# Banded attention ahead of two feed-forward blocks: scores on 64 by 64 quarters of the array, row sums by a unit column

## The chip, the cores and the metric

The kernel runs on one core of a Trainium2 chip. The metric is the device time of one execution in microseconds (us). Times are medians over executions; the profile is of one execution.

## The reference

Attention over 2 batches of 8 heads, 768 positions of 64 dimensions. Each query sees the keys less than 16 positions away, and 24 summaries of the whole sequence (the maximum of each block of 32 keys, the mean of each block of 32 values). Two feed-forward blocks follow.

```python
k_sum = k.reshape(B, H, nb, 32, D).max(axis=3)
v_sum = v.reshape(B, H, nb, 32, D).mean(axis=3)
scores_l = where(|i - j| < 16, scale * q @ k.T, -1e9)
scores_s = scale * q @ k_sum.T + log(32)
a = softmax(concatenate([scores_l, scores_s]))      # a / (sum(a) + 1e-9)
x = a @ concatenate([v, v_sum])                     # 1536 rows x 512
x = x / rms(x) * rms_g
x = (silu(x @ w_gate) * (x @ w_val)) @ w_out        # 512 -> 1536 -> 512
x = (s * relu(x @ w_in) ** 2 + b) @ w_out2          # 512 -> 2048 -> 512
```

## The kernel before

**Tiles.** The 1536 rows (2 batches of 768) are 12 tiles of 128 queries, numbered 0 to 11; tiles 0 to 5 are batch 0. A tile has two halves of 64 queries, and each half sees 96 keys of its own window and the 24 summaries: KC = 120 columns of scores for each of 8 heads. The 8 heads are two groups of four, so there are 24 units of work, one for each tile and group.

**Scores (L587).** The two halves of a tile see different keys. On the SBUF partitions the keys of the first half are in rows 0 to 63 and those of the second half in rows 64 to 127. The queries come from DRAM already laid out with zeros (`qz`): for each head a 128 by 128 block, in which one half of the queries has its dimensions in the upper 64 rows and zeros below, the other the reverse. One matrix product of depth 128 for each head then gives 128 queries by 120 scores. Half of `qz` is zeros: 24 loads of 256 KB.

**The rest of a unit.** VectorE adds the mask and takes the row maximum, head by head (`do_top`, L597, tile `P`). ScalarE takes the exponential and with it the row's sum (`do_exp`, L604). TensorE turns the four heads (L615) into a PSUM bank, ScalarE copies that to `PT` (L634), TensorE multiplies with the values (L644). GpSimd makes the reciprocal of the sums (L621, L622, a power of -1), and VectorE multiplies by it (L651) into `xn`. When both units of a tile are there, ScalarE takes the sum of squares (L670), GpSimd its power of -1/2 (L675, L676), VectorE scales the row (L678), TensorE turns it (L686), and ScalarE and VectorE write it as a high and a low part into `x` (L699, L701).

**Summaries.** VectorE reduces the keys (L292), copies halves across (L297), and ScalarE or GpSimd spreads them beside the keys (L303, L305). The means of values are summed on VectorE (L332), turned on TensorE (L345) and copied beside some windows of values (L352, L354); 18 transfers within SBUF (L357) take them to the other windows.

**Feed-forward.** Weights come as pairs of words and are rebuilt on ScalarE, VectorE (L218 to L220) and GpSimd (L235), then split in two parts. A product of one block of weights with 512 rows of `x` is 12 matrix products of 512 columns (`mm12`, L786, L787, L790). The first 6 weights of the first block run in the attention's time, once for each of three blocks of 512 rows (tiles 0 to 3, 4 to 7, 8 to 11): 18 such products. All else follows them, in an order of its own.

**Order of the work.** `plan` lists tasks with an engine, an assumed duration, dependences and a rank, and `give_out` hands them out by a simulated clock: at each moment each free engine takes the lowest rank that is ready. The result is a fixed order on each engine, and on the chip each engine takes its instructions strictly in that order. Where the simulated TensorE would be idle for more than 0.6 us, four transpositions of the identity (L459) are put in its order. PSUM's 8 banks are shared by purpose (`caps`: 3 for scores, `S`).

## Time and profile before

| what | value |
|---|---|
| median of 3 executions | 649.98 us (648.75 to 651.63) |
| the profiled execution, its own time | 650.19 us |
| its span from first to last instruction | 648.4 us |
| TensorE busy | 626.2 us (97%) |
| VectorE, ScalarE, GpSimd busy | 383.0, 269.0, 155.4 us |
| DMA | 59.4 MB, mean 92 GB/s |

The profiled execution took 1.8 us more than its span. A busy time is a share of the whole span, over stages that differ: the attention lies in the first 110 us or so, and TensorE's products of the feed-forward blocks fill the rest.

### The profile page before, as it was taken

What the parts mean: (1) busy time and instruction counts of PE and PEld (TensorE: products, weight loads), DVE (VectorE), ACT (ScalarE), POOL (GpSimd) and SP (SyncE); (2) the same over time, 40 slices, a digit from 0 to 9 for tenths busy, and PEclk for the clock granted to TensorE, in tenths of its full rate; (3) what the DMA queues carried; (4) which work ended last, traced back from release to release, by engine and by line L of the source; (5) the groups of instructions that cost most, each with busy time, mean ns of one, the idle gap of its engine ahead of it and who ended that gap; (6) DMA issues with size and microseconds to landing.
All of it is one profiled execution on the core that took longest, in us unless ns stands there. A gap on an engine that the chain in (4) does not pass through costs nothing.

```text
span 648.4 us, 8708 instructions
## 1 busy us (share of the span) xinstructions
PE 626.2 (97%) x3232; PEld 518.9 (80%) x3232; DVE 383.0 (59%) x754; ACT 269.0 (41%) x615; POOL 155.4 (24%) x187
## 2 busy tenths in 40 slices
PE   4788989999999999999999999999999999999997
PEld 3577877888888888888888888888888888888886
DVE  4589987225861555644556667870388548845532
ACT  3797996233443333211333335542454045404400
POOL 3456884332221111111111111100221022102100
PEclk9999999999999999999999999999999999999999
DMA  9998942003340211111111111121111211110022
GB/s 283 273 300 272 257 152 98 1 0 98 110 139 11 66 65 66 66 65 66 65 66 65 66 66 65 66 91 40 46 53 65 98 64 44 62 59 2 0 98 97
DMA packets 20930, 59.38 MB, mean 92 GB/s; under 512 B 2664, under 2 KB 2920, under 8 KB 20888
## 3 DMA queue, kind: packets, MB, share of 16 engines
q1 hardware_dynamic: 20888, 58.83, 28.0%
q8 instruction: 25, 0.41, 0.3%
q14 instruction: 17, 0.14, 0.1%
HBM read 54.79 MB, written 3.15 MB: 89 GB/s over the span
## 4 chain that ended last, share of the span: by engine, by line
PE 88%; ACT 4%; DVE 3%; DMA 2%; POOL 1%; issue 1%; SPq 0%; DVEq 0%
PE b L786 21%; PE b L790 21%; PE b L787 21%; PE b L910 7%; PE b L912 7%; PE b L909 7%; ACT P L604 2%; PE b L587 2%; DMA qz<-in_q_t_dram 1%; DMA hg<-in_k_t_dram 1%; PE b L644 1%; ACT PT L634 1%; PE b L615 1%; DVE xn L678 0%; PE b L686 0%
## 5 line engine op out<-in xcount | busy, mean ns | idle before, releaser
L235 POOL TENSOR_TENSOR wl<-wa,wh 128x512 fp32r<-128x512 f32 x68 | 89.8, 1327 | 387.0 <-ACT wh L231 313.8
L786 PE MATMUL b<-x,wh 128*128 128x512 f32 x288 | 113.5, 394 | 0.1
L787 PE MATMUL b<-x,wl 128*128 128x512 f32 x288 | 112.3, 390 | 0.0
L231 ACT ACTIVATE wh<-wa 128x512 fp32r<-128x512 f32 x68 | 41.5, 626 | 96.6 <-PE b L912 45.5
L790 PE MATMUL b<-x,wh 128*128 128x512 f32 x288 | 77.7, 392 | 0.0
L910 PE MATMUL b<-wl,hg 128*128 128x512 f32 (+1 forms) x196 | 75.2, 385 | 0.0
L909 PE MATMUL b<-wh,hg 128*128 128x512 f32 (+1 forms) x196 | 75.2, 385 | 0.0
L787 PE MATMUL b<-y,wl 128*128 128x512 f32 x192 | 74.8, 390 | 0.0
L786 PE MATMUL b<-y,wh 128*128 128x512 f32 x192 | 74.8, 390 | 0.0
L891 DVE SCALAR_TENSOR_TENSOR b<-u,sbc 128x512 f32<-128x512 f32 x48 | 50.7, 1056 | 35.6 <-ACT u L890 35.6
L786 PEld LDWEIGHTS b<-x,wh 128*128 128x128 f32 x288 | 54.1, 188 | 11.2 <-ACT x L699 0.2
L787 PEld LDWEIGHTS b<-x,wl 128*128 128x128 f32 x288 | 54.2, 188 | 10.8
L790 PEld LDWEIGHTS b<-x,wh 128*128 128x128 f32 x288 | 53.6, 188 | 10.8
L787 PE MATMUL b<-hg,wl 128*128 128x512 f32 x144 | 56.1, 390 | 0.0
L786 PE MATMUL b<-hg,wh 128*128 128x512 f32 x144 | 56.1, 390 | 0.0
L220 DVE SCALAR_TENSOR_TENSOR wa<-raw,wa 128x512 int32<-128x512 int32 x68 | 52.4, 770 | 2.0
L811 DVE SCALAR_TENSOR_TENSOR hg<-b,bbc,hg 128x512 fp32r<-128x512 f32 x48 | 36.0, 749 | 28.2 <-ACT hg L810 28.2
L912 PE MATMUL b<-wh,hg 128*128 128x512 f32 (+1 forms) x196 | 51.5, 385 | 0.0
L790 PE MATMUL b<-y,wh 128*128 128x512 f32 x192 | 51.3, 390 | 0.0
L810 ACT ACTIVATE hg<-b,bbc 128x512 fp32r<-128x512 f32 x48 | 33.0, 688 | 42.8 <-DVE b L891 42.8
L918 DVE TENSOR_TENSOR part<-b,part 128x512 f32<-128x512 f32 (+1 forms) x37 | 24.4, 673 | 43.4 <-PE b L912 43.4
L219 DVE SCALAR_TENSOR_TENSOR wa<-raw,wa 128x512 int32<-128x512 int32 x68 | 47.4, 697 | 2.0
(94 smaller groups left out, 975.3 us busy)
## 6 DMA issues: line engine op xcount, KB each, us to landing
raw<-in_w_out_dram SPq DMA_DIRECT2D x28, 512.0 KB
raw<-in_w_in_dram SPq DMA_DIRECT2D x16, 512.0 KB
qz<-in_q_t_dram SPq DMA_DIRECT2D x24, 256.0 KB
raw<-in_w_gate_dram SPq DMA_DIRECT2D x12, 512.0 KB
raw<-in_w_val_dram SPq DMA_DIRECT2D x12, 512.0 KB
vt<-in_v_t_dram SPq DMA_DIRECT2D x8, 384.0 KB
hg<-in_k_t_dram SPq DMA_DIRECT2D x5, 576.0 KB
out_dram<-part SPq DMA_DIRECT2D x11, 256.0 KB
```

What stands on the lines that cost most here:

```text
L219: lambda: nc.vector.scalar_tensor_tensor(out=ai, in0=hi, scalar=-0x80000000, in1=ai, op0=ALU.bitwise_and, op1=ALU.bitwise_or),
L220: lambda: nc.vector.scalar_tensor_tensor(out=ai, in0=lo, scalar=29, in1=ai, op0=ALU.logical_shift_right, op1=ALU.bitwise_or),
L231: nc.scalar.activation(out=r(h), in_=a_t[i], func=AF.Copy)
L235: nc.gpsimd.tensor_tensor(out=r(lo), in0=a_t.pop(i), in1=high[i], op=ALU.subtract)
L786: nc.tensor.matmul(ps, r(hi[:, kk * 128:(kk + 1) * 128]), xh, start=kk == 0, stop=False)
L787: nc.tensor.matmul(ps, r(lo[:, kk * 128:(kk + 1) * 128]), xh, start=False, stop=False)
L790: nc.tensor.matmul(ps, r(hi[:, kk * 128:(kk + 1) * 128]), r(act(kk, 1)), start=False, stop=kk == 3)
L811: nc.vector.scalar_tensor_tensor(out=r(dst[1]), in0=ps, scalar=bias, in1=dst[0], op0=ALU.add, op1=ALU.subtract)
L891: after(0, lambda u=u, ps=ps: nc.vector.scalar_tensor_tensor(out=ps, in0=u, scalar=sbc[:, 0:1], in1=u, op0=ALU.mult, op1=ALU.mult))
L909: nc.tensor.matmul(acc, gh, r(ws[e][0][:, cs]), start=e == 0, stop=False)
L910: nc.tensor.matmul(acc, gh, r(ws[e][1][:, cs]), start=False, stop=False)
L912: nc.tensor.matmul(acc, r(ge[e][:, 1]), r(ws[e][0][:, cs]), start=False, stop=e == 3)
```

## The change

- Scores (now L595): the queries come without zeros (`q`, 12 loads of 256 KB, three buffers instead of two). A head's two halves are two products of depth 64, 64 queries by 120 columns each. Even heads go to PSUM partitions 0 to 63 and odd ones to 64 to 127, each half of the tile to a bank of its own, so the four products of a pair of heads lie on the four 64 by 64 quarters of the array. A tile's scores are now one task of 16 products, which needs the keys of all 8 heads, and a unit is now a half of a tile with all 8 heads, no longer a group of heads with both halves. `S` may hold 4 banks, and there are 4 buffers `PT` instead of 2.
- Values have 66 columns for each head, of which two are set to one by GpSimd (`ones_v`): the product with the values (L656) then gives the row's sum in columns 64 and 65. It needs `PT` of both halves. The exponential (L622) no longer sums; ScalarE copies the sums out of PSUM and adds 1e-9 (`do_sum`, L668, 24 of them), and GpSimd takes one power of 8 columns for each tile (L672).
- Loads of values are one contiguous piece each; means are spread by 5 transfers instead of 18; the vectors `rms_g`, `s`, `b` come as one load, already repeated for 128 rows. In `do_top` the masks of the first and the last half differ from the others. In the other lines only numbers moved (L678 is L695, L686 is L703, L701 is L718, L786 is L803, L787 is L804, L790 is L807, L597 is L615, L615 is L633, L634 is L643, L459 is L464).

```diff
+QB = 3
-    RINGS = {"P": 3, "PT": 2, "u": 2, "vs": 1}
+    RINGS = {"P": 3, "PT": 4, "u": 2, "vs": 1}
-    qz = [const.tile([128, 2, GH, 128], F32, name=f"qz{i}") for i in range(2)]
+    qc = [const.tile([128, NH, HQ], F32, name=f"q{i}") for i in range(QB)]
-        nc.sync.dma_start(out=t, in_=v_w[b, :, s0:s0 + n])
+        nc.sync.dma_start(out=t.rearrange("p s h d -> p (s h d)"), in_=v_w[b, s0 // n])
+
+    def ones_v(b, s0, n):
+        rows = KC if s0 < (4 if b == 0 else 2) else KW
+        nc.gpsimd.memset(vst[b][s0 // NTL][0:rows, s0 % NTL:s0 % NTL + n, :, HD:VH], 1.0)
-    caps = {"S": 3, "T": 2, "X": 3, "M": 3}
+    caps = {"S": 4, "T": 2, "X": 3, "M": 3}
-                    VM[b, t, "ok"] = [task("SP", 0.3, lambda s=s: spread_v(b, s), first, 2 * (6 * b + t) - 6) for s in (2 * t, 2 * t + 1)]
+                    if t in (1, 2 if b == 0 else 1, 3):
+                        n = 6 if t == 3 else 2 if b == 0 else 4
+                        spr = task("SP", 0.3 * n, lambda t=t, n=n: spread_v(b, 2 * t, n), [*first, O[b, 0]], 2 * (6 * b + t) - 6)
+                    VM[b, t, "ok"] = [spr]
-        us = [(i, g) for g in range(2) for i in range(2)] + [(i, g) for i in range(2, NT) for g in range(2)]
+        us = [(i, c) for i in range(NT) for c in range(2)]
+            def do_qk(bk):
+                box["S", i, 1] = bank(bk)
+                sm_of[i] = smallp.tile([128, 2, NH], F32, tag="sm", name="sm")
+                for h in range(NH):
+                    j, o = divmod(h, 2)
+                    for c in range(2):
+                        p = slice(64 * c, 64 * c + 64)
+                        nc.tensor.matmul(box["S", i, c][64 * o:64 * o + 64, j * KC:(j + 1) * KC].rearrange("p (r c) -> p r c", c=CH),
+                                         qc[i % QB][p, h], kst[b][h // GH][p, h % GH, :, t], start=True, stop=True)
+            deps = [Q[i], *[o for h in range(NH) for o in KM[b, h]], *([qk[i - 1]] if i else ())]
-                for j in range(GH):
-                    h = GH * g + j
-                    nc.tensor.matmul(ps[:, j * KC:(j + 1) * KC].rearrange("p (r c) -> p r c", c=CH),
-                                     qz[i % 2][:, g, j], kst[b][g][:, j, :, t], start=True, stop=True)
-                                     bias=sm_of[i][:, 0, h:h + 1], accum_out=sm_of[i][:, 1, h:h + 1])
+                                     bias=sm_of[i][:, 0, h:h + 1])
-            ex = [task("ACT", 0.38, lambda j=j, f=do_exp: f(j), [tops[j]], n + 0.5 + j * 0.01) for j in range(GH)]
+            ex = [task("ACT", 0.29, lambda j=j, f=do_exp: f(j), [tops[j]], n + 0.5 + j * 0.01) for j in range(GH)]
+            def do_sum(u, i=i):
+                xv = box["X", i, u][:, 0:GH * VH].rearrange("p (h d) -> p h d", h=GH)
+                nc.scalar.activation(out=sm_of[i][:, 1, GH * u:GH * u + GH].rearrange("p (h o) -> p h o", o=1), in_=xv[:, :, HD:HD + 1],
+                                     func=AF.Identity, bias=tiny[:, 0:1])
+            def do_rc(i=i):
+                nc.gpsimd.tensor_tensor(out=sm_of[i][:, 1], in0=sm_of[i][:, 1], in1=mone, op=ALU.pow)
+            for u in range(2):
+                C.append(task("PE", 0.62, lambda bk, u=u, f=do_pv: f(bk, u), [PTS[i, 0], pt, O[b, t], *VM[b, t, "ok"], *C],
+                              n + 0.2, bank="X", give=(("PT", PTS[i, 0]), ("PT", pt)) if u else ()))
+                U.append(task("ACT", 0.2, lambda u=u, f=do_sum: f(u), [C[u]], n + 0.0))
+            RC = task("POOL", 1.6, do_rc, U, n - 1)
+            for u in range(2):
+                N.append(task("DVE", 0.36, lambda u=u, f=do_norm: f(u), [RC, *N], n + 0.0, free=(C[u],), take=() if u else ("xn",)))
```

Three places show how the order of work moves. The first is the start of TensorE's order, before: `hg` and `kx` are buffers of keys (heads 0 to 3 and 4 to 7 of batch 0), `qz_103` and `qz_104` the queries of tiles 0 and 1, `vt` sums of values, `b` a PSUM bank.

```order
L587 MATMUL b_198<-hg,qz_103 128x120 x4
L587 MATMUL b_204<-hg,qz_104 128x120 x4
L459 MATMUL b_219<-ident 128x128 x4
L345 MATMUL b_228<-ident,vt 128x128 x2
L459 MATMUL b_236<-ident 128x128 x4
L615 MATMUL b_248<-ident,P 120x128 x4
L459 MATMUL b_263<-ident 128x128 x4
```

And in the changed kernel, from the last of 7 groups of identity transpositions on, through the scores of tile 0 (8 products on `hg`, 8 on `kx`, `q_102` being the queries of tile 0):

```order
L464 MATMUL b_246<-ident 128x128 x4
L464 MATMUL b_253<-ident 128x128 x4
L464 MATMUL b_263<-ident 128x128 x4
L348 MATMUL b_271<-ident,vt 128x128 x2
L595 MATMUL b_277<-hg,q_102 64x120
L595 MATMUL b_278<-hg,q_102 64x120
...
L595 MATMUL b_277<-kx,q_102 64x120
L595 MATMUL b_278<-kx,q_102 64x120
...
L595 MATMUL b_300<-hg,q_103 64x120
L595 MATMUL b_303<-hg,q_103 64x120
```

The first scores stood first in the order; now they stand behind the turn of the second pair of sums of values (L348), and tile 0 has all 8 heads there at once, where heads 4 to 7 came behind ten other entries.

The second place is VectorE's order ahead of the first scaling of a row (L678, L695: tile 0), before (`b_373` to `b_441` are products with the values of tiles 0 and 1, `b_427` is a bank of scores of tile 2, ISA rows of `sm` alone read out an accumulator):

```order
L651 TENSOR_TENSOR xn<-b_373,sm 128x256
L651 TENSOR_TENSOR xn<-b_388,sm 128x256
L651 TENSOR_TENSOR xn<-b_412,sm 128x256
L597 ISA P,sm<-b_427,mask_97 128x120
L597 ISA sm 128x1
...
L651 TENSOR_TENSOR xn<-b_441,sm 128x256
...
L678 SCALAR_TENSOR_TENSOR xn<-xn,ss,gbc 128x512
```

And in the changed kernel (`b_351` holds scores of tile 2, `b_403` and `b_423` tile 0's products with the values, `b_478` and `b_494` scores of tile 3):

```order
L615 ISA P,sm<-b_351,mask_98 128x120
L615 ISA sm 128x1
L664 TENSOR_TENSOR xn<-b_403,sm 128x256
L664 TENSOR_TENSOR xn<-b_423,sm 128x256
L615 ISA P,sm<-b_478,mask_98 128x120
...
L615 ISA P,sm<-b_494,mask_98 128x120
...
L695 SCALAR_TENSOR_TENSOR xn<-xn,ss,vec 128x512
```

Both multiplications by the reciprocal (L664) now stand together, behind 24 maxima (tiles 0 to 2), and four maxima of tile 3 stand between them and the scaling.

The third place is TensorE's order where the second block of 512 rows begins its products (before: L786 on `b_1370`; `qz_104` is here tile 11's queries):

```order
L587 MATMUL b_1316<-hg,qz_104 128x120 x4
L686 MATMUL b_1328<-ident,xn 128x128 x4
L644 MATMUL b_1336<-part,PT 64x64 x8
L615 MATMUL b_1353<-ident,P 120x128 x4
L587 MATMUL b_1361<-hg,qz_104 128x120 x4
L786 MATMUL b_1370<-x,wh 128x512
L787 MATMUL b_1370<-x,wl 128x512
...
L644 MATMUL b_1385<-part,PT 64x64 x8
```

And in the changed kernel (`b_1541` is the same product, `b_1519` and `b_1595` turn the rows of tiles 8 and 9, `b_1578` turns the first half of tile 11):

```order
L595 MATMUL b_1494<-hg,q_104 64x120
L703 MATMUL b_1519<-ident,xn 128x128 x4
L656 MATMUL b_1527<-part,PT 64x66 x8
L803 MATMUL b_1541<-x,wh 128x512
L804 MATMUL b_1541<-x,wl 128x512
...
L656 MATMUL b_1552<-part,PT 64x66 x8
...
L633 MATMUL b_1578<-ident,P 120x128 x4
L807 MATMUL b_1541<-x,wh 128x512 x4
L703 MATMUL b_1595<-ident,xn 128x128 x4
```

The scores of tile 11 stand just ahead in both. Before, three units were still to be turned and four still to be multiplied with the values from the first L786 of this product on; now two and three.

## Rows read from the trace of the kernel before

**Rows 1.** Busy time by stretch of the span: stretch and length, then each engine's busy us
```profile
0.00:20.50 20.50, 10.48 (x50) 7.57 (x50) 10.88 (x41) 8.97 (x31) 7.98 (x34) 1.00 0.94 296
20.50:34.00 13.50, 10.44 (x114) 8.94 (x115) 7.43 (x41) 9.19 (x40) 4.53 (x8) 0.89 1.00 237
34.00:52.70 18.70, 16.26 (x194) 14.03 (x192) 16.60 (x55) 15.98 (x54) 12.63 (x19) 0.99 0.93 323
52.70:94.60 41.90, 38.55 (x377) 32.65 (x377) 37.81 (x146) 37.50 (x138) 32.74 (x46) 1.00 0.80 229
94.60:648.40 553.80, 550.48 (x2503) 455.66 (x2501) 310.30 (x475) 197.35 (x355) 97.53 (x82) 1.00 0.18 62
```

**Rows 2.** TensorE in order of time: four marks (start us, us, what, idle before)
```profile
20.54 2.05 PE L587 MATMUL b<-kx,qz 128*128 128x120 f32 x16
...
30.55 1.60 PE L587 MATMUL b<-kx,qz 128*128 128x120 f32 x8 [2.52 <-DMA qz<-in_q_t_dram]
...
52.75 0.50 PE L786 MATMUL b<-x,wh 128*128 128x512 f32 x1
...
94.60 0.48 PE L786 MATMUL b<-x,wh 128*128 128x512 f32 x1
```

**Rows 3.** The same view: scores, a transposition and a value product, each with what follows
```profile
34.03 2.18 PE L587 MATMUL b<-hg,qz 128*128 128x120 f32 x16
36.05 1.06 PE L587 MATMUL b<-kx,qz 128*128 128x120 f32 x8
...
37.38 0.60 PE L615 MATMUL b<-ident,P 128*120 128x128 f32 x4
37.81 0.60 PE L686 MATMUL b<-ident,xn 128*128 128x128 f32 x4
...
45.24 0.69 PE L644 MATMUL b<-hg,PT 120*64 120x64 f32 x16
45.86 0.77 PE L615 MATMUL b<-ident,P 128*120 128x128 f32 x4
```

**Rows 4.** Waits between 52.7 and 94.6 us: TensorE's longest (total, times, longest us)
```profile
PE b L686 <- DVE xn L678: 1.8, 2, 1.5
```

**Rows 5.** VectorE in order of time, 0 to 110 us
```profile
33.89 0.75 DVE L678 SCALAR_TENSOR_TENSOR xn<-xn,ss,gbc 128x512 f32<-128x512 f32 x1
...
57.04 0.74 DVE L678 SCALAR_TENSOR_TENSOR xn<-xn,ss,gbc 128x512 f32<-128x512 f32 x1
57.70 0.94 DVE L292 TENSOR_REDUCE ks<-hg 128x24 f32<-128x768 f32 x1
...
61.28 0.95 DVE L332 TENSOR_REDUCE vs<-vt 128x24 f32<-128x768 f32 x1
62.14 0.42 DVE L651 TENSOR_TENSOR xn<-b,sm 128x256 f32<-128x256 f32 x1
62.47 0.68 DVE L219 SCALAR_TENSOR_TENSOR wa<-raw,wa 128x512 int32<-128x512 int32 x1
63.07 0.28 DVE L597 CUSTOM_DVE_ANT_0 P<-b,mask 128x120 f32<-128x120 f32 x1
63.27 0.69 DVE L220 SCALAR_TENSOR_TENSOR wa<-raw,wa 128x512 int32<-128x512 int32 x1
...
66.90 1.58 DVE L220 SCALAR_TENSOR_TENSOR wa<-raw,wa 128x512 int32<-128x512 int32 x1
```

**Rows 6.** VectorE in order of time, 74 to 115 us: tile 8's scaling
```profile
91.23 0.75 DVE L678 SCALAR_TENSOR_TENSOR xn<-xn,ss,gbc 128x512 f32<-128x512 f32 x1 [0.72 <-POOL ss L676]
```

**Rows 7.** ScalarE in order of time: one exponential, its sum, the next
```profile
70.28 0.39 ACT L604 ACTIVATE P<-P,sm 128x120 f32<-128x120 f32 x1
70.57 0.19 ACT L604 ACTIVATION_READ_ACCUMULATOR P<-P,sm 128x1 f32 x1
70.66 0.39 ACT L604 ACTIVATE P<-P,sm 128x120 f32<-128x120 f32 x1
```

**Rows 8.** GpSimd in order of time: powers of 4 and of 1 columns, a subtraction
```profile
16.27 1.07 POOL L622 TENSOR_TENSOR sm<-sm,mone 128x4 f32<-128x4 f32 x1
...
31.07 0.56 POOL L676 TENSOR_TENSOR ss<-ss,mhalf 128x1 f32<-128x1 f32 x1
...
66.19 1.74 POOL L770 TENSOR_TENSOR hg<-u,hg 128x512 fp32r<-128x512 f32 x1
```

**Rows 9.** SyncE's queue in order of time: spreading the means (issues)
```profile
27.68 6.21 SPq L357 DMA_DIRECT2D hg<-hg  x6
...
75.50 9.72 SPq L357 DMA_DIRECT2D part<-part  x10
```

More of the change, by code (lines that the diff above doesn't have):

```diff
@@ L57, with kernel @@
 @with_exitstack
-def kernel(ctx: ExitStack, tc: tile.TileContext, q_t, k_t, v_w, v_t, w_gate, w_val, w_out, w_in2, w_out2, rms_g, s2, b2, out):
+def kernel(ctx: ExitStack, tc: tile.TileContext, q_t, k_t, v_w, v_t, w_gate, w_val, w_out, w_in2, w_out2, vecs, out):
     nc = tc.nc
@@ L546, in means @@
                 pairs = slice(2 * g, 2 * g + 2)
-                sums = [task("DVE", dve(768), lambda pr=pr: sum_vt(b, pr), [VT[b, pr], z], rank + 1.5 * g,
-                             give=(("raw", VT[b, pr]),) if b else ()) for pr in (2 * g, 2 * g + 1)]
+                sums = [task("DVE", dve(768), lambda pr=pr: sum_vt(b, pr), [VL[b, pr], z], rank + 1.5 * g,
+                             give=(("raw", VL[b, pr]),) if b else ()) for pr in (2 * g, 2 * g + 1)]
                 tv = task("ACT", 0.54, lambda pairs=pairs: turn_vs(b, pairs), sums, rank + 1.5 * g)
@@ L576, in plan @@
+        PTS = {}
         for n, (i, g) in enumerate(us):
             b, t = divmod(i, NTL)
-            if g == 0 and i >= 2:
-                lq(i, (n - 5, n - 4.9), [qk[i - 2, 0], qk[i - 2, 1]])
-            def do_qk(bk, i=i, g=g, b=b, t=t):
-                ps = box["S", i, g] = bank(bk)
-                if i not in sm_of:
-                    sm_of[i] = smallp.tile([128, 2, NH], F32, tag="sm", name="sm")
-                for j in range(GH):
-                    h = GH * g + j
-                    nc.tensor.matmul(ps[:, j * KC:(j + 1) * KC].rearrange("p (r c) -> p r c", c=CH),
-                                     qz[i % 2][:, g, j], kst[b][g][:, j, :, t], start=True, stop=True)
@@ L589, in plan @@
-            deps = [Q[i, g], *[o for j in range(GH) for o in KM[b, GH * g + j]]]
-            A = qk[i, g] = task("PE", 0.82, do_qk, deps, n + 1.2, bank="S", take=("sm",) if g == 0 else ())
+            if g == 0:
+                holds = tile_of(n, i)
+            A, A1 = holds[g], holds[1]
             def do_top(j, i=i, g=g, t=t):
@@ L690, in plan @@
             if i == 2 * TPS:
-                deps += [qk[j, 1] for j in range(NTL)]
+                deps += [qk[j] for j in range(NTL)]
             ET = task("PE", 0.44, do_e, deps, n - 1, bank="M", give=(("xn", box["N0", i]),))
@@ L943, in _layout @@
     c = np.ascontiguousarray
-    qt = np.zeros((NB, NTL, 2, HD, NH, 2, HQ), np.float32)
-    for h in range(2):
-        qt[:, :, h, :, :, h] = q.reshape(NB, NH, NTL, 2, HQ, HD)[:, :, :, h].transpose(0, 2, 4, 1, 3)
-    qt = qt.reshape(NT, 128, 2, GH * 128)
+    qt = q.reshape(NB, NH, NTL, 2, HQ, HD).transpose(0, 2, 3, 5, 1, 4).reshape(NT, 128, NH * HQ)
     own = np.arange(HQ) + WIN
```

146 lines of the change are left out of this document (68 added, 78 removed).

## The prediction

> **What bounds the kernel now.** I first cut the span where TensorE's work changes its kind [rows 1, 2]. At 20.54 us the scores of heads 4 to 7 begin, at 52.75 the first product of the feed-forward block, at 94.60 the second block of 512 rows. From there to the end TensorE is busy 550.48 of 553.8 us: nothing in that stretch can be shortened by attention, so the change can only move the moment at which TensorE reaches that point, and the little attention that is still left behind it. Everything is decided in the first 94.6 us.
>
> There no single engine is the bound. From 52.7 to 94.6 TensorE is busy 38.55 of 41.9 us, VectorE 37.81, ScalarE 37.50, GpSimd 32.74 [rows 1]. TensorE waits for little, and most of it for VectorE's scaling of a row (1.8 us in two waits [rows 4]). From 34 to 52.7 VectorE is busy 16.60 of 18.7. Before 34 everything waits for keys and queries: DMA's share is 0.94 and 1.00, VectorE is busy about half, and TensorE stood 2.52 us for queries at 30.55 [rows 1, 2]. So I read this as three engines, each near nine tenths, in strict orders; what counts is the work that stands ahead of TensorE's second block on each of them.
>
> **The change, part by part.**
>
> *Scores on TensorE.* Sixteen passes of the old scores take 36.05 - 34.03 = 2.02 us, 0.126 us each; a product is two passes, so 96 products cost 192 x 0.126 = 24.2 us [rows 3]. Now there are 192 products, 384 passes. The trace has no pass on a quarter. The nearest row is the value product, whose two halves already lie on two column halves of the array: 16 passes of 64 columns in 45.86 - 45.24 = 0.62 us, 0.039 us each [rows 3]. Lower bound: a quarter's pass costs that too, 384 x 0.039 = 15.0 us, 9 less. Upper bound: four quarters run in turn and each pass costs the old 0.126: 48.4 us, 24 more. A middle one scales the value pass by its columns, 120/64 x 0.039 = 0.073: 28 us, 4 more. I take 0.05 (19 us, 5 less), nearer to the value row, because that row shows that parts of the array overlap, and here four products lie on four parts and two banks.
> The Trainium skill (TensorEngine Tiling, Key Properties) says that tiles execute in parallel, which agrees with the value row; by it alone scores would come to about half of before. The same section says that a change of tiling mode drains the engine; that speaks against the change, which enters and leaves the mode once for each of 12 tiles, and no row here gives its price; what it may cost stands with the rivals.
>
> *Exponentials.* One takes 70.66 - 70.28 = 0.38 us with its sum, of which the read of the sum is the last 0.09 (it starts at 70.57) [rows 7]. Without the sum I take 0.29: 96 x 0.09 = 8.6 us less. Added are 24 copies of sums out of PSUM, which I price between the 0.09 of such a read and the 0.29 of an exponential, at 0.2: 4.8 us. ScalarE gains 4 us of the 72 that it is busy ahead of 94.6 [rows 1], no more.
> The Trainium skill (ScalarE: Activation LUTs, What ACT_TABLE_LOAD costs) lets a bias read per partition, which both the exponential and the new copy have, add about 93 ns to an instruction; by that the 0.29 stays, as I took it, and with a cheaper exponential it would be a larger gain.
>
> *GpSimd.* A power of 4 columns took 1.07 us, of one column 0.56 [rows 8]: 0.17 a column, so 8 columns cost about 1.75. 24 powers of 1.07 become 12 of 1.75, 25.7 us become 21; the 24 additions ahead of them go, and 12 small settings of ones come. But the reciprocal now starts only when both halves have been multiplied with the values and their sums copied; before it ran beside the turning and the copy. One tile's way from maxima to scaling grows by the sum copies and the power, 2 us, and in the order of GpSimd the power of the next tile stands behind the scaling's power of this one.
>
> *DMA.* 24 loads of 256 KB become 12: 3.1 MB, at the 237 to 323 GB/s of the early stretches [rows 1] 10 us of DMA. VectorE, TensorE and ScalarE hide nearly all of it after 34 us; ahead of that it takes away the 2.52 us wait [rows 2] and about 0.9 us (one 256 KB load) ahead of the keys of heads 4 to 7. The 18 spreads, 6 of which held SyncE's queue for 6.21 us and 10 for 9.72 [rows 9], become 5; TensorE's waits name none of them, so I price this at nothing; if a spread came late, tile 1's or tile 7's value products would stand behind it. The contiguous values and the single load of vectors I price at nothing for the same reason: the loads of values were not waited for.
>
> *The order.* The first scores stand behind the second pair of sums of values and need all keys. So the 4 heads of tiles 0 and 1 that were done by 20.54 come later: TensorE and ScalarE lose that start, VectorE 8 maxima (8 x 0.20 = 1.6 us).
>
> **The sum.** It goes by VectorE, the busiest of the waiting engines in both stretches from 34 to 94.6. Its instructions start after one another, in a row without gaps, by: maximum 0.20, multiplication (L651) 0.33, scaling 0.66, reduction of 768 0.86, one step of weights (L219, L220) 0.60 [rows 5]; the short step L218 I take at 0.34, `x` and the gate's steps at 0.60, small copies at 0.18 and copies of means at 0.42.
> 1. Tile 0's scaling starts at 33.89 before [rows 5]. Now: keys complete at about 19.7 (20.54 less 0.9), scores of a tile 1 us, first maximum at 21. Then 8 maxima 1.6, last exponential 0.4, two turns 0.9 (37.81 - 37.38 = 0.43 each [rows 3]), two copies and the exponentials of tile 1 between them 2.5, value products 1.2, sums 0.4, power 1.75, two multiplications 0.7, squares and their power 1.6: 11. It starts at about 32.5, between 30.5 and 34.5, and ends 0.7 later.
> 2. From there to the last maximum of tile 11's first half, VectorE now has, counted in its order: 65 maxima (13.0), 18 multiplications (5.9), 9 short and 16 long steps of weights (12.7), 9 writes of `x` and 6 gate steps (9.0), 8 reductions (6.9), 8 scalings (5.3), 6 copies (1.5): 54.3 us. Before, from the end of tile 0's scaling to the end of tile 8's (34.6 to 92.0 [rows 5, 6]), it had 46.0 us by the same prices (59, 14, 6 and 12, 7 and 4, 8, 8, 6) in 57.4: 11.4 us went into gaps and into instructions that GpSimd stretched (1.58 us for a step of 0.60 while a subtraction of 1.74 ran [rows 5, 8]). GpSimd has about as many of these subtractions ahead as before, some 8, so 6 us of it stay; the gaps, 5, shrink as TensorE and ScalarE have less to do. I take 9 in all: 63.3 us, and 33.2 + 63.3 = 96.5. The exponential and its wait add 0.8: TensorE turns tile 11's first half at 97.3.
> 3. Behind that: the 553.8 us of before, less one turn (0.43) and one value group (0.62) that are now done earlier, less what stands between the second block's first product and this turn: 8 products at 0.22 (550.48 us over 2503 [rows 1]) and a value group, 2.4. That leaves 550.3.
> Span: 97.3 + 550.3 = 647.6, against 648.4: 0.8 us less. The profiled execution took 650.19 around its span, 0.2 above the median 649.98, so the forecast is a median of 649.2, which I call no change. A half per cent, 3.25 us, is about what a measurement of this kernel tells from no change.
>
> **The rivals.**
> *A larger gain.* The gaps of VectorE nearly vanish, since TensorE (5 us less of scores in the stretch at the lower bound), ScalarE and the queues all give way. With 5 us in place of 9, and tile 0's scaling at 31.5: 5 us earlier, a span of 642.6, median 644.2. For it: VectorE's busy share can be full where its order is filled, and rows 4 show that TensorE waits for it. Against: ScalarE keeps 95% of its work. Chance 0.32.
> *VectorE gets no faster.* The same share of gaps as before, 46.0 in 57.4, makes 67.8 out of 54.3: 101.8 with step 1 and the 0.8, span 652.1, median 653.7. The mechanism is the longer way through GpSimd to the scaling: if each of 8 tiles waits 0.5 us more, it is reached. Chance 0.13.
> *Quarters in turn: slower.* From 52.7 on 6 tiles of scores stand ahead of the second block, 192 passes. TensorE has 3.35 us free in that stretch [rows 1], gives up 96 old passes (12.1) and takes on two turns and three value groups more (2.7). So 192 p - 12.1 + 2.7 > 3.35 from p = 0.066 us on: from there TensorE is the bound. At 0.126 that is 11.4 us over, of which the later end that I forecast hides 2.7: some 8 or 9 more, median 658. A price on each change between the whole array and quarters would act in the same place: at 0.05 a pass the three terms come to 0.2, so 3.15 us stay for 12 changes in this stretch, and from 0.26 us each on TensorE is the bound. Chance of both 0.11. (The drain of the Trainium skill, cited above, is that mechanism.)
> *The change does nothing where it counts:* the scores' gain falls wholly into waits. That is the forecast's own neighbourhood and is in its chance.
>
> **Chances and range.** The forecast, with gaps and stretching between 6.5 and 12, runs from 646.7 to 652.2 by median, which is also its own range, and has 0.44, all of it within the half per cent. The larger gain makes faster 0.32, the two slow rivals slower 0.24. To leave out no more than 2 in 10 it must take in most of the larger gain and of the rival without faster VectorE, and of the quarters in turn only the near end: 643 to 655.
>
> **What the changed profile would show.** Scores: 32 passes of a tile in 1.2 to 1.9 us; over 2.3 and the rival of the turns holds. The first L595 near 20, the first L695 near 32.5, the turn of tile 11's first half (L633, the last but one) near 97. Exponentials 0.29 apart. VectorE over 92% busy from 52 to 95. TensorE idle 8 us more than before ahead of that turn, nearly all of it ahead of 21 us and in waits for L615, L622 or L695; none named after the spreads. The prediction is wrong if TensorE's waits in that stretch name the sums or the power (L668, L672), or if the products of the second block have gaps.

## The result, and the profile after

The changed kernel takes 658.59 us (median of 4 executions, 658.19 to 659.63) against 650.2 us for the kernel before (4 executions): a ratio of 1.0146 (95% interval 1.0124 to 1.0167; the plain quotient of the two medians is 1.0129). It is slower by 8.4 us, on the other side of the forecast and outside its range. The profiled execution took 658.19 us, with a span of 656.4 us; that of before had 648.4.

The stretches of [rows 1], with the last one up to the new end (columns as there):

```profile
0.00:20.50 20.50, 7.36 (x27) 4.96 (x28) 10.98 (x26) 4.80 (x15) 5.50 (x32) 1.00 0.92 288
20.50:34.00 13.50, 12.64 (x190) 9.97 (x191) 6.25 (x51) 10.09 (x33) 2.25 (x6) 1.00 1.05 220
34.00:52.70 18.70, 14.43 (x228) 11.02 (x222) 15.88 (x52) 14.22 (x40) 9.92 (x16) 1.00 1.05 314
52.70:94.60 41.90, 37.77 (x420) 29.59 (x421) 37.40 (x130) 33.21 (x94) 22.22 (x30) 0.92 0.61 172
94.60:656.40 561.80, 558.71 (x2600) 457.87 (x2600) 314.28 (x498) 201.90 (x366) 100.90 (x81) 1.00 0.19 61
```

Over the first four stretches together no engine is busier than before (TensorE is in the second, ScalarE in the second too). The loss shows when the same point of the work is looked for in both: the 300th matrix product of the feed-forward blocks starts at 157.70 us before and at 160.55 after, and from there to the end it takes 490.7 and 495.85 us. So 2.85 of the 8.0 us of span are lost in the attention and 5.15 behind it, in a stretch that the forecast held to be unchanged.

TensorE in order of time, answering to [rows 2, 3]:

```profile
13.27 8.10 PE L464 MATMUL b<-ident 128*128 128x128 f32 x28
...
22.06 1.08 PE L595 MATMUL b<-hg,q 64*64 64x120 f32 x16
...
54.63 0.63 PE L703 MATMUL b<-ident,xn 128*128 128x128 f32 x4 [2.09 <-DVE xn L695]
...
57.14 0.80 PE L803 MATMUL b<-x,wh 128*128 128x512 f32 x1 [0.63 <-ACT x L716]
...
65.30 0.65 PE L633 MATMUL b<-ident,P 128*120 128x128 f32 x4
65.88 1.05 PE L595 MATMUL b<-hg,q 64*64 64x120 f32 x32
66.86 0.69 PE L656 MATMUL b<-hg,PT 120*64 120x66 f32 x16
...
72.24 0.65 PE L633 MATMUL b<-ident,P 128*120 128x128 f32 x4
72.65 0.48 PE L803 MATMUL b<-x,wh 128*128 128x512 f32 x1
...
106.94 0.60 PE L633 MATMUL b<-ident,P 128*120 128x128 f32 x4
```

The scores themselves did what was wanted: 32 passes take 66.86 - 65.88 = 0.98 us, 0.031 each, against 0.126 before. The first product of the blocks starts at 57.14 instead of 52.75. VectorE's first maximum and first scaling, answering to [rows 5]:

```profile
24.02 0.28 DVE L615 CUSTOM_DVE_ANT_0 P<-b,mask 128x120 f32<-128x120 f32 x1 [1.02 <-PE b L595]
...
37.55 0.75 DVE L695 SCALAR_TENSOR_TENSOR xn<-xn,ss,vec 128x512 f32<-128x512 f32 x1
```

Up to that 300th product TensorE's time can be balanced. The view by stretch (columns as in [rows 1]), of before and then of after: all work, then the instructions of two source lines alone, identity transpositions and scores (of those the first two columns, TensorE and its weight loads, are to be read):

```profile
0.00:157.70 157.70, 138.79 (x1071) 114.64 (x1072) 103.92 (x342) 96.88 (x319) 77.88 (x128) 0.99 0.58 175
0.00:157.70 157.70, 7.17 (x44) 5.46 (x44) 0.99 0.58 175
0.00:157.70 157.70, 28.38 (x192) 25.52 (x192) 0.99 0.58 175
```
```profile
0.00:160.55 160.55, 138.14 (x1295) 109.09 (x1296) 105.54 (x342) 92.18 (x247) 63.22 (x105) 0.98 0.54 154
0.00:160.55 160.55, 15.33 (x76) 10.53 (x76) 0.98 0.54 154
0.00:160.55 160.55, 13.99 (x384) 11.36 (x384) 0.98 0.54 154
```

Scores gave back 28.38 - 13.99 = 14.4 us. Transpositions of the identity, put in where the plan left TensorE idle, took 8.2 of it, and TensorE stands idle 22.4 us instead of 18.9. In the same view the products with the values take 17.72 us instead of 16.03, and the three lines of the blocks' 300 products together 2.8 more, since part of them ran at half clock (last section). So most of what scores gave up went into filling and waiting, and some into slower work.

### The profile page after: what moved, and what is told of

It reads as the page before. It is cut to its first block, busy times and chain, and to the rows that moved or that the text cites. A ratio compares the mean times of both kernels' runs of the same rounds, so it can differ in the third digit from the quotient of the medians.

```text
span 656.4 us, 8987 instructions
## 1 busy us (share of the span) xinstructions
PE 630.9 (96%) x3456; PEld 513.4 (78%) x3456; DVE 384.8 (59%) x754; ACT 264.2 (40%) x543; POOL 140.8 (21%) x164
## 4 chain that ended last, share of the span: by engine, by line
PE 90%; DMA 4%; DVE 2%; ACT 1%; issue 1%; SPq 0%; POOL 0%; ACTq 0%
PE b L803 22%; PE b L807 21%; PE b L804 21%; PE b L929 7%; PE b L926 7%; PE b L927 7%; DMA raw<-in_w_val_dram 2%; DMA part<-in_v_w_dram 2%; DMA vt<-in_v_t_dram 1%; PE b L464 1%; PE b L656 1%; PE b L595 1%; PE b L633 1%; DVE P L615 1%; ACT P L622 0%
## 5 line engine op out<-in xcount | busy, mean ns | idle before, releaser
L803 PE MATMUL b<-x,wh 128*128 128x512 f32 x288 | 114.6, 398 | 0.6 <-ACT x L716 0.6
L804 PE MATMUL b<-x,wl 128*128 128x512 f32 x288 | 113.2, 393 | 0.0
L807 PE MATMUL b<-x,wh 128*128 128x512 f32 x288 | 78.3, 394 | 0.0
L926 PE MATMUL b<-wh,hg 128*128 128x512 f32 (+1 forms) x196 | 76.2, 390 | 0.0
L804 PE MATMUL b<-y,wl 128*128 128x512 f32 x192 | 74.7, 389 | 0.0
L803 PE MATMUL b<-y,wh 128*128 128x512 f32 x192 | 74.7, 389 | 0.0
L908 DVE SCALAR_TENSOR_TENSOR b<-u,vec 128x512 f32<-128x512 f32 x48 | 50.7, 1057 | 36.6 <-ACT u L907 36.6
L803 PEld LDWEIGHTS b<-x,wh 128*128 128x128 f32 x288 | 54.6, 190 | 12.1 <-ACT x L716 1.0
L804 PEld LDWEIGHTS b<-x,wl 128*128 128x128 f32 x288 | 54.7, 190 | 10.9
L807 PEld LDWEIGHTS b<-x,wh 128*128 128x128 f32 x288 | 54.0, 190 | 11.1
L803 PE MATMUL b<-hg,wh 128*128 128x512 f32 x144 | 56.7, 394 | 0.0
L804 PE MATMUL b<-hg,wl 128*128 128x512 f32 x144 | 56.5, 392 | 0.0
L929 PE MATMUL b<-wh,hg 128*128 128x512 f32 (+1 forms) x196 | 52.9, 392 | 0.0
L828 DVE SCALAR_TENSOR_TENSOR hg<-b,vec,hg 128x512 fp32r<-128x512 f32 x48 | 36.0, 749 | 28.2 <-ACT hg L827 28.2
L807 PE MATMUL b<-y,wh 128*128 128x512 f32 x192 | 51.3, 389 | 0.0
L827 ACT ACTIVATE hg<-b,vec 128x512 fp32r<-128x512 f32 x48 | 33.0, 687 | 42.8 <-DVE b L908 42.8
```

The costliest lines, as they stand in the source:

```text
L803: nc.tensor.matmul(ps, r(hi[:, kk * 128:(kk + 1) * 128]), xh, start=kk == 0, stop=False)
L804: nc.tensor.matmul(ps, r(lo[:, kk * 128:(kk + 1) * 128]), xh, start=False, stop=False)
L807: nc.tensor.matmul(ps, r(hi[:, kk * 128:(kk + 1) * 128]), r(act(kk, 1)), start=False, stop=kk == 3)
L828: nc.vector.scalar_tensor_tensor(out=r(dst[1]), in0=ps, scalar=bias, in1=dst[0], op0=ALU.add, op1=ALU.subtract)
L908: after(0, lambda u=u, ps=ps: nc.vector.scalar_tensor_tensor(out=ps, in0=u, scalar=sbc[:, 0:1], in1=u, op0=ALU.mult, op1=ALU.mult))
L926: nc.tensor.matmul(acc, gh, r(ws[e][0][:, cs]), start=e == 0, stop=False)
```

## The experiments

**The stretch behind the attention.** Theory: a line of the change that the forecast did not price. Windows of values with 66 columns need 3168 columns in a buffer, and the five buffers `hg` later hold the hidden layers of the blocks:

```diff
-        return hgp.tile([128, NSUB * 2 * SUB], F32, tag="hg", name="hg")
+        return hgp.tile([128, VT], F32, tag="hg", name="hg")
```

That is 3072 columns before and 3168 now. A group of 12 products that read `hg`, from its first product to the next group's (before, then after):

```profile
291.21 0.39 PE L786 MATMUL b<-hg,wh 128*128 128x512 f32 x1
...
293.93 0.39 PE L786 MATMUL b<-hg,wh 128*128 128x512 f32 x1
```
```profile
292.39 0.40 PE L803 MATMUL b<-hg,wh 128*128 128x512 f32 x1
...
295.17 0.40 PE L803 MATMUL b<-hg,wh 128*128 128x512 f32 x1
```

2.72 against 2.78 us. From 140 us on the mean distance of starts of all such products is 226.7 ns before and 232.0 after; products that read `x` or `y` stand 226.7 apart in both. The trace has 996 on `hg`: 996 x 5.3 ns = 5.3 us, which is the 5.15 found above. The rival is that the products are slower for the order or for TensorE's clock. Two runs, one from each side:

```diff
 # pad_hg, the changed kernel:
-        return hgp.tile([128, VT], F32, tag="hg", name="hg")
+        return hgp.tile([128, 3584], F32, tag="hg", name="hg")[:, 0:VT]
 # before_wide_hg, the kernel before (a scratch buffer is made smaller for room, as in the changed kernel):
+        return hgp.tile([128, 3168], F32, tag="hg", name="hg")[:, 0:NSUB * 2 * SUB]
```

> The changed kernel with one edit: each tile hg is allocated with 3584 columns and only its first 3168 are used. No instruction moves. Layout theory: the feed-forward products that read hg on either side (996 of them, 432 of the first block's output and 564 of the second's) stand 232.0 ns apart in the changed kernel and 226.7 ns in the kernel before, where the tile had 3072 columns; products that read x or y stand 226.7 ns apart in both. If the place of the tiles in a partition does that, 3584 columns (a multiple of 512, as 3072 is) give 226.7 ns back, 996 x 5.3 ns = 5.3 us: 653.3 us. Rival, all of the loss lies in the attention (late first scores and GpSimd's waits): 658.6 us, and the spacing stays at 232. A second rival, the spacing comes from the memory that the change moved elsewhere (weights and x also lie at other places): the spacing stays too.

> The kernel before with one edit, the converse: tiles hg of 3168 columns instead of 3072, of which 3072 are used (and, to make room, the same small DMA scratch that the changed kernel has). Layout theory: products that read hg go from 226.7 to about 232 ns apart, 5.3 us more, 655.5 us, with the attention as it was. Rival, the loss lies in the attention alone: 650.2 us.

Beside the kernel before at 649.03, pad_hg took 653.28 (1.007, 1.0048 to 1.0093) and before_wide_hg 654.26 (1.0085, 1.0051 to 1.012). A stretch in which TensorE is busy throughout, in the order before, after, pad_hg, before_wide_hg:

```profile
140.00:620.00 480.00, 480.00 (x2119) 397.76 (x2118) 281.15 (x416) 177.04 (x305) 78.83 (x60) 1.00 0.18 63
```
```profile
140.00:620.00 480.00, 480.00 (x2099) 394.08 (x2098) 279.21 (x413) 176.11 (x304) 78.99 (x61) 1.00 0.19 62
```
```profile
140.00:620.00 480.00, 480.00 (x2119) 397.50 (x2118) 282.05 (x418) 177.17 (x305) 78.86 (x60) 1.00 0.18 62
```
```profile
140.00:620.00 480.00, 480.00 (x2099) 394.26 (x2098) 279.25 (x413) 176.73 (x305) 78.84 (x60) 1.00 0.18 62
```

In equal time and at a granted clock of 1.00, the two kernels with 3168 columns do 2099 products and the two others 2119. In the profiled executions of all twenty kernels of this case the stretch from the 300th product of the blocks to the end takes 490.5 to 490.7 us, except for the four with 3168 columns (the changed kernel, before_wide_hg and the next two, ones_loaded and no_early_fill), where it takes 495.8 to 496.0. The size of the buffer alone, without a change of order, gives and takes the 5.3 us: this is shown. (Beside its own kernel before, the changed kernel's excess falls only from 8.4 to 4.2 us, because that kernel took 649.03 beside pad_hg and 650.2 beside the changed kernel.) By which property of an address it acts is open; 3072 and 3584 columns are multiples of 512, 3168 is not, and `x` and `y` lie elsewhere too, without effect.

**GpSimd's ones and the early transpositions.** Padded, the kernel is still 4.2 us over. In the changed kernel's list of waits between 20 and 106 us (total, times, longest us) the first and the third are GpSimd's settings of ones behind loads of values:

```profile
POOL hg L285 <- DMA hg<-in_v_w_dram: 18.3, 5, 7.5
...
POOL part L285 <- DMA part<-in_v_w_dram: 8.9, 5, 3.4
```

Theory: powers that stand behind them come late. In ones_loaded the ones come with the values, and GpSimd sets only the rows of the means, early. A second theory is that the 28 transpositions at 13.27 us keep scores from starting; in no_early_fill none is put in before the first scores.

```diff
 # ones_loaded
-        rows = KC if s0 < (4 if b == 0 else 2) else KW
-        nc.gpsimd.memset(vst[b][s0 // NTL][0:rows, s0 % NTL:s0 % NTL + n, :, HD:VH], 1.0)
+        nc.gpsimd.memset(vst[b][s0 // NTL][KW:KC, s0 % NTL:s0 % NTL + n, :, HD:VH], 1.0)
+    vw[..., HD:VH] = 1.0
```

> The changed kernel with the ones coming in with the loaded values; GpSimd sets only those of the summary rows, early and without a wait for a load. Theory of GpSimd's waits: in the changed kernel GpSimd stands 33.6 us in 11 waits for value loads, with powers queued behind them. For tile 0 the last such wait ends at 32.05, only 0.4 us after tile 0's sums are there; for tile 3 it holds the row's power from 51.7 to 52.9. So tile 0's scaling comes 0.4 us earlier, tile 3's 1 to 1.5, and the first feed-forward product at about 55.6 instead of 57.14: 1 to 2.5 us less, 656 to 657.6 us. What I held right after the result, that these waits are nearly the whole loss, would give 651 to 652. Rival, the start and the longer way through the sums set all: under 0.5 us, 658.1 to 658.6 us.

> The changed kernel without transpositions of the identity ahead of the first scores (28 of them, 8.10 us, end at 21.4, while the last spread of keys ends at 20.66). Theory of the late start: first scores at 20.7 to 21.0 instead of 22.06, first maximum 1 to 1.3 us earlier, tile 0's scaling too: 0.8 to 1.5 us less, 657.1 to 657.8 us. Rival, those transpositions were what brought TensorE's clock up, and without them scores and turns run longer at the lower level: no gain or up to 1.5 us more, 658.6 to 660 us.

ones_loaded took 659.76 (1.0163): no gain, the theory fell. VectorE, GpSimd and TensorE there, at the scaling of tile 3:

```profile
52.54 0.95 DVE L294 TENSOR_REDUCE ks<-hg 128x24 f32<-128x768 f32 x1
53.41 1.29 DVE L694 SCALAR_TENSOR_TENSOR xn<-xn,ss,vec 128x512 f32<-128x512 f32 x1
```
```profile
52.16 0.54 POOL L692 TENSOR_TENSOR ss<-ss,mhalf 128x1 f32<-128x1 f32 x1
52.88 1.26 POOL L234 TENSOR_TENSOR wl<-wa,wh 128x512 fp32r<-128x512 f32 x1 [0.18 <-DMA q<-in_q_t_dram]
```
```profile
54.84 0.63 PE L702 MATMUL b<-ident,xn 128*128 128x128 f32 x4 [2.17 <-DVE xn L694]
```

GpSimd's power is done at 52.70, yet the scaling that TensorE waits for starts at 53.41: here it stands behind a reduction in VectorE's own order. It then takes 1.29 us instead of the usual 0.75, while GpSimd, freed from its wait, runs a subtraction. In the changed kernel this scaling waited 0.36 us for the power, started at 53.73 and took 0.75: it ended at 54.48, here at 54.70. no_early_fill took 656.81 (1.0124); its first scores start at 20.88 instead of 22.06. How large its gain is stays unclear: 1.8 us by the medians, but only 0.6 if each is taken against the executions of the kernel before that stood beside it (7.8 us over 649.03 against 8.4 over 650.2), where 0.8 to 1.5 was expected.

**The rest, from the changed kernel's side.** All these have the padded `hg`. Two further edits are combined with no_early_fill's: `recip` replaces the GpSimd power by VectorE's reciprocal, which shortens the way from sums to scaling, and `halves` gives the scores of tiles 0 and 1 in two tasks, heads 0 to 3 as soon as their keys are there.

```diff
-                nc.gpsimd.tensor_tensor(out=sm_of[i][:, 1], in0=sm_of[i][:, 1], in1=mone, op=ALU.pow)
+                nc.vector.reciprocal(sm_of[i][:, 1], sm_of[i][:, 1])
...
+            A1 = task("PE", 0.5, do_qk, [*deps, A0], rk, bank="S", take=("sm",))
+            A2 = qk[i] = task("PE", 0.5, lambda: do_qk(None, range(NH // 2, NH)),
```

> Both edits that gave time back, together: tiles hg of 3584 columns and no transpositions of the identity ahead of the first scores. They act in different stretches, so they should add: 653.3 less 1.8 = 651.5 us (650.7 to 652.3). Rival, the earlier start was worth something only by chance of where TensorE's clock fell (it stood at 0.50 from 57 to 63 us in the changed kernel, not in the one with padded tiles): 653 us.

> As the run above it, and the reciprocal of the 8 sums by VectorE in place of GpSimd's power. Theory of the longer way through GpSimd: from tile 1 on the power of a tile (1.65 us) starts only when the row's power of the tile ahead is done, that one waits for the squares, these for the multiplication, and this for the power: a ring of about 4 to 6 us a tile, and the rows of tiles 0 to 3 are turned at 39.3, 43.4, 48.5, 54.6 in the changed kernel (36.9, 37.8, 44.0, 51.4 before). Without the power in it tile 0 is 1.5 us earlier and each further one up to 1: the first product 2 to 4 us earlier, 648 to 650 us in all. Rival, VectorE's and ScalarE's orders and the loads set the pace and the ring only fills gaps: under 0.7 us, 650.8 to 651.5 us.

> As the first of these, and the scores of tiles 0 and 1 in two tasks each, heads 0 to 3 as soon as their keys are there (about 5 to 13 us, as before), heads 4 to 7 when theirs are; the maxima of the first two pairs of heads follow the first task. Theory that the late first scores (which now need the keys of all heads) cost: VectorE has 8 of its first 16 maxima, 1.6 us, behind it and ScalarE 8 exponentials, 2.3 us, when the keys of heads 4 to 7 come, so tile 0's scaling comes 1.5 to 2.5 us earlier, 649 to 650.5 us. Rival, TensorE's later start at the low clock or the order behind eats it: 651 to 651.5 us.

> All of the edits above together. If the late start and the way through GpSimd are both causes, it is 646 to 648.5 us, faster than the changed kernel by 10 to 12 and than the kernel before by 1 to 3. If only one is, 648 to 650. If neither, 651.

Beside 648.62 they took 653.08 (1.0055), 652.32 (1.0046), 652.77 (1.0055) and 652.36 (1.0058); every interval excludes 1.002 and none reaches the expected gain. pad_nofill did not add up, and 653.08 is where its rival (653) put it, whose mechanism, the clock, this run does not show. In its profiled execution, at 656.80 the slowest of ten, tile 3's queries came late, a wait that the changed kernel has at 1.34 us; that explains this execution, not the median:

```profile
40.00 1.08 PE L595 MATMUL b<-hg,q 64*64 64x120 f32 x16 [3.81 <-DMA q<-in_q_t_dram]
```

Four more: pad_all has all of these, a fourth buffer of queries and later loads of batch 1's values; pad_all_warm is that with the threshold for identity transpositions at 0.3 us instead of 0.6; pad_old_loads takes back the loads and spreads of before; pad_three_undone is padded, with halves, recip and the old loads.

```diff
-QB = 3
+QB = 4
-            lv(1, t, 9 + t)
+            lv(1, t, 12.5 + 1.5 * t)
-IDLE = 0.6
+IDLE = 0.3
```

> The changed kernel with tiles hg of 3584 columns, no early transpositions of the identity, scores of tiles 0 and 1 in two tasks, VectorE's reciprocal, and two edits to the order of loads: a fourth buffer for queries, so that tile 3's load no longer waits for tile 0's scores (it was waited for 1.3 to 3.8 us), and batch 1's values later in the queue, so that the weights of the first products come ahead of them (a weight was waited for 3.2 us in the last of the runs with halves and reciprocal). If loads are what ate the gains of the other edits, 646 to 649 us; if not, 651 to 653 as those runs.

> The run with all edits (pad_all, 653.05 us; 649.35 in the execution whose granted clock was 1.00, up to 657.94 in those at 0.99), with transpositions of the identity put in where the planner sees 0.3 us of idle time instead of 0.6. If the clock at the first feed-forward products is what spoils it, fewer executions fall below 0.995 and the median comes to 649 to 651; if these transpositions do not hold the clock, or delay work, 653 or more.

> The changed kernel with tiles hg of 3584 columns and the transfers as before: values in pieces of two slots out of a longer row, 18 spreads of means, three loads of the vectors. If the transfers cost as much here as they did on the kernel before (3.0 us), 650 to 651 us; if something else covers them, as with the edits that gave single causes back, 652.5 to 653.5.

> As the run above it, and the scores of tiles 0 and 1 in two tasks (first heads early) and the reciprocal on VectorE: all three parts that cost time on the kernel before undone, with the quarters, the unit column and the cheaper exponentials kept. If these three are the rest of the loss, 646 to 649 us, at the kernel before or ahead of it; if the rest has another cause, 651 to 653.

pad_all took 653.05 (649.35 to 657.94; before 648.93; 1.0074, 1.0043 to 1.0105). Beside 649.38, pad_all_warm took 652.02 (1.0044), pad_old_loads 655.18 (1.0083) and pad_three_undone 652.26 (1.0047). No part that was undone gave the 4 us back, singly or with others; pad_old_loads came out above both of the ranges named for it.

**The rest, from the side of the kernel before.** One trait of the change at a time: before_late (scores of tiles 0 and 1 wait for the keys of all heads, and the units go tile after tile, a second edit that is not in the diff below), before_long_way (one reciprocal of 8 columns for a tile, behind both products with the values), before_loads (contiguous values, merged spreads, one load of vectors), and the first two together.

```diff
-            deps = [Q[i, g], *[o for j in range(GH) for o in KM[b, GH * g + j]]]
+            deps = [Q[i, g], *[o for h in (range(NH) if i < 2 else range(GH * g, GH * g + GH)) for o in KM[b, h]]]
...
+            rc = task("POOL", 1.85, do_rc, [*ex0, *ex, C0, C], n - 1)
```

> The kernel before with one edit: the scores of tiles 0 and 1 wait for the keys of all 8 heads, as in the changed kernel (there because four products share the array). With tiles hg padded the changed kernel is still some 4.4 us slower than the one before (653.1 to 648.7), and edits that gave single causes back in it moved nothing beyond 1 us. Theory of the late start: VectorE has 8 maxima (1.6 us) and ScalarE 8 exponentials (3 us) behind the keys of heads 4 to 7 at 20.5 instead of ahead of them; 1.5 to 4 us more, 650.2 to 652.6 us. Rival, the waits for queries at 30.55 (2.52 us) hide it: under 0.7 us more.

> The kernel before with one edit: one addition and one power of 8 columns for each tile, and only after both value products of the tile (24 powers of 4 columns, beside the turning, before); sums still come from the exponential. Theory of the long way through GpSimd: 2.0 us between the products and the multiplication in each of the first 4 tiles, partly covered by VectorE's other work: the first feed-forward product 1 to 3 us later, 649.7 to 651.7 us. Rival, VectorE is the bound and has other work to do: under 0.7 us.

> The kernel before with the edits of the change to its transfers alone: values as contiguous pieces, means spread by 5 transfers instead of 18, one load of the vectors. Forecast of mine: nothing (648.0 to 649.3 us). Rival: the merged spreads hold the queue ahead of the loads of queries (at 23.08 in the changed kernel, with tile 3's queries behind it and waited for 1.34 us) and it is 1 to 2 us slower; or the 13 fewer issues free the queue and it is 1 to 2 faster.

> The kernel before with late first scores and the long way of the sums together. If each acts on its own, 648.9 + 6.5 + 5.4 = 660.8 us; if they overlap (both delay the scaling of the first four tiles, and VectorE has other work while it waits), 655 to 658.

They cost 6.5 us (655.43, 1.0115), 5.4 us (654.37, 1.0095), 3.0 us (651.91, 1.005) and 10.5 us (659.86, 1.016). The first three cost more than was expected of them, and the two together nearly the sum of both. Read alone, each of these would pass for a cause. But each also gives the planner other numbers, and so another order everywhere. The control for that changes one assumed duration in the plan of before and no work of the kernel; only the number of identity transpositions, which the planner itself puts in, moves with the order (52 and 36 instead of 44):

```diff
 # before_plan_exp
-            ex = [task("ACT", 0.38, lambda j=j, f=do_exp: f(j), [tops[j]], n + 0.5 + j * 0.01) for j in range(GH)]
+            ex = [task("ACT", 0.34, lambda j=j, f=do_exp: f(j), [tops[j]], n + 0.5 + j * 0.01) for j in range(GH)]
 # before_plan_scores
-            A = qk[i, g] = task("PE", 0.82, do_qk, deps, n + 1.2, bank="S", take=("sm",) if g == 0 else ())
+            A = qk[i, g] = task("PE", 1.0, do_qk, deps, n + 1.2, bank="S", take=("sm",) if g == 0 else ())
```

> The kernel before with one number of its plan changed, the assumed duration of an exponential, 0.34 us instead of 0.38: the same instructions on the same data, only their order on the engines differs. Order theory: the order of before is a good one among many, and another one costs 2 to 5 us, as much as the part of the loss that is left: 651 to 654 us. Rival, the order that the planner gives is about equally good for close numbers, and the rest of the loss belongs to the parts of the change: 648.6 to 650 us.

> The kernel before with another number of its plan changed, the assumed duration of the scores of four heads, 1.0 us instead of 0.82. Order theory: again 2 to 5 us slower, 651 to 654 us. Rival: 648.6 to 650 us.

They took 653.62 (1.0076, 1.0058 to 1.0095) and 654.08 us (1.0072, 1.0046 to 1.0097) beside 649.38: 4.2 and 4.7 us for another order with its filling. In the first of them the blocks even begin earlier than before (52.75 in [rows 2]), and the loss comes between there and the 300th product (160.80 us instead of 157.70):

```profile
51.15 0.47 PE L786 MATMUL b<-x,wh 128*128 128x512 f32 x1
```

So an effect of 3.0 us on that side can't be told from a re-planned order, nor, with two controls alone, one of 5.4; 6.5 and 10.5 are larger than either control. The 4.2 us that the padded kernel has left are as large as the controls.

## Why the prediction was wrong

**The step that failed** and weighs most against the kernel before is the third: "the 553.8 us of before, less one turn". It held that the products behind the attention keep their price. 996 of them rose from 226.7 to 232.0 ns because their operand's buffer grew from 3072 to 3168 columns: 5.3 of the 8.4 us, shown from both sides. The width of the values was read as work (66 columns in a product) and not as the size of a buffer that other products read later.

**A second error in that step hid the first.** The 94.60 in [rows 2] was taken for the second block of 512 rows; it is the fifth product of the first block. Nor is `b_1541` in the changed kernel's order the same product as `b_1370`, as was held: it is the seventh, the first of the second block. Counting one line in the stretch of before up to there, and in the changed kernel up to its corresponding mark at 104.15, shows it:

```profile
L786 PE MATMUL b<-x,wh 128*128 128x512 f32 x17 | 7.4, 435 | 0.1
```
```profile
L803 PE MATMUL b<-x,wh 128*128 128x512 f32 x24 | 11.1, 463 | 0.6 <-ACT x L716 0.6
```

A product has four of these, so four products had run before, and six run now ahead of that mark. By prices of before the rest behind tile 11's turn should have been 24 x 0.227 = 5.4 us less than the 550.3 forecast: 544.9. It measured 656.4 - 106.94 = 549.5 and looked right, since the slower products put back nearly the same. With the mark set right the sum gives 642.2 instead of 647.6, and the measured 656.4 is 14.2 us above it: 5.0 in the start, 4.6 in the stretch that went by VectorE, 4.6 behind tile 11's turn.

**Start (step 1).** Tile 0's scaling came at 37.55, not 32.5, outside its own bounds of 30.5 to 34.5. The first maximum came at 24.02 instead of 21: the turn of the value sums and 28 identity transpositions stand ahead of the first scores, and those took 0.80 per 16 passes up to about 25.3. The last us of the delay is order: GpSimd has the row's power ready at 36.49, but four maxima of tile 3 stand ahead of the scaling, and they wait for tile 3's scores, which waited 1.34 us for queries:

```profile
35.94 0.55 POOL L693 TENSOR_TENSOR ss<-ss,mhalf 128x1 f32<-128x1 f32 x1
```
```profile
36.73 0.28 DVE L615 CUSTOM_DVE_ANT_0 P<-b,mask 128x120 f32<-128x120 f32 x1 [2.15 <-PE b L595]
```

The DMA share is 1.05 from 20.5 to 52.7, where a relief was forecast.

**VectorE (step 2).** From the end of that scaling to tile 11's turn 68.7 us passed (38.2 to 106.9), where 64.1 were forecast (63.3 to the last maximum, and 0.8). The rival "VectorE gets no faster" had 68.6 here. It named 653.7 us, and the padded kernel has 653.28; that is luck, for the rival had the early start too, some 5 us that did not come, and the wrong mark, 5.4 us the other way. Its mechanism, the longer way through GpSimd, is not shown: recip shortened it and won 0.8 us at most. Nor was VectorE the bound from the first product to that turn. TensorE, which has six products there instead of four, is busy 48.25 of 49.80 us, 5.9 of them at half clock, and VectorE 44.90 (columns as in [rows 1]):

```profile
57.10:106.90 49.80, 48.25 (x576) 37.81 (x577) 44.90 (x169) 43.10 (x123) 25.82 (x29) 0.94 0.49 144
```

**What held.** Scores are cheaper than the lower bound of 0.039: 0.031 a pass. The turn ahead of scores takes 65.88 - 65.30 = 0.58 us, ahead of a product 72.65 - 72.24 = 0.41: 0.17 for an entry into quarters. Leaving them costs less: 16 passes take 0.52 us ahead of a turn (27.14 to 27.66) and 0.46 ahead of more passes (26.68 to 27.14). Both are below the 0.26 from which TensorE would be the bound by these changes. So the rival of quarters in turn, with a price for entering them, is wrong, though its 658 us is what was measured: luck, by another cause. 12 entries cost some 2 us, and 14.4 were gained. The Trainium skill (TensorEngine Tiling (Array Packing), Key Properties) says that tiles work in parallel and that changing the mode drains the engine. The trace agrees with the first by 0.031 us a pass; with the second the 0.17 us is in line, but no row here shows a drain as such. Exponentials stand 0.29 apart, as forecast, and GpSimd's power of 8 columns takes 1.65 (1.75 forecast, [rows 8]). The signs of being wrong that were named did not appear: TensorE's waits name neither the sums nor the power, and the second block's products have no gaps. One wait of 0.26 us is for a spread of means, which was priced at nothing. The cause that was found lay outside these signs.

**What stays open.** The other 3 to 4 us lie ahead of the 300th product, in the attention. The controls show that another order can cost as much; that the order is what costs it here is argued, not shown. TensorE's idle time ahead of 26 us grew from 10.2 to 13.3 us. The clock's half rate moves single executions (beside pad_all_warm the kernel before has a median of 648.55 us in three executions at a mean granted clock of 1.00, and 651.94 in four at 0.992), but it is not what is left: at equal clocks the distance stays, 653.53 (5 executions of pad_hg) against 649.66 (7 of the kernel before) at 0.997, and 651.72 (6 of pad_all_warm) against 648.55 (3) at 1.00. Which wait it is could not be settled: undoing a single part re-plans everything, and in both controls that alone moved the time by 4 us. No version ran faster than the kernel before.

## What to carry to other kernels

Look in a diff for sizes of buffers as well as for instructions, and compare the distance of the same products in both traces in the stretch that "cannot have changed": 5 ns on a thousand products was the larger part here. Where a planner turns durations into a fixed order, run a control that changes a number in the plan alone; an effect no larger than that (4.2 and 4.7 us here) cannot be put down to an edit. And check that a mark in one trace is the same piece of work in the other, by counting instructions up to it.

## What the runs showed of the hardware

- The size of the tile in which a matrix product's operand lies changed the product's rate: products of 512 columns stood 226.7 ns apart with tiles of 3072 (the kernel before) and 3584 columns (pad_hg), 232.0 ns with 3168 (the changed kernel, before_wide_hg), whichever side of the product the tile was on.
- In the changed kernel's profiled execution TensorE had no matrix product for 2.09 us ahead of 54.63; from 57.10 to 63.00 the granted clock was 0.50 (its level of 1.2 GHz), and products of the block stood 0.43 apart instead of 0.23. The kernel before has the same behind its wait of 2.52 us ahead of 30.55. In pad_hg's execution, with 1.63 us of idle time ahead of 54.41, the products stood 0.23 apart at a granted clock of 1.00 (2.4 GHz). The changed kernel's stretch without a product and the one behind it, then a stretch of the kernel before:

```profile
52.60:54.60 2.00, 0.00 (x0) 0.00 (x1) 1.61 (x3) 0.37 (x2) 1.29 (x5) 1.00 1.07 259
57.10:59.00 1.90, 1.86 (x4) 1.39 (x5) 1.90 (x7) 0.80 (x4) 0.12 (x1) 0.50 1.06 245
```
```profile
32.10:34.00 1.90, 1.90 (x21) 1.78 (x21) 1.35 (x10) 1.38 (x7) 0.00 (x0) 0.50 0.69 173
```

- The 28 transpositions of the identity at 13.27 us stood 0.29 apart for 8.1 us, and the scores behind them took 0.80 per 16 passes until about 25.3 us and 0.46 after it, although the rows give a granted clock of 1.00 there. The four at 28.15 stood 0.11 apart. What set the early rate is not shown.
